# Attention steps of the next group spread over nine tenths of a group's MoE, with a larger planned sum of their matmuls

## The chip, the cores and the metric

The kernel runs on one core of one Trainium2 chip. The metric is the device time of one execution in microseconds, the median over several. A core has a matrix engine (TensorE, PE in the profile), a vector engine (VectorE, DVE), an activation engine (ScalarE, ACT), a general-purpose engine (GpSimd, POOL) and a queue engine (SyncE, SP). Each has its own instruction stream, and streams wait for one another through semaphores. Matmul results go to PSUM, from where ACT and DVE read them.

## The reference

Two stages: attention over 4 batches, 8 heads, 768 positions and head size 64, then a mixture of four experts (MoE) on its output.

```python
scores = scale * np.matmul(q, k.transpose(0, 1, 3, 2))
# retrieval heads 0, 2, 6: causal mask; the other five ("streaming" heads):
# causal and (key among the first 4, or within the last 64 positions)
a = softmax(where(mask, scores, -1e9))
attn = np.matmul(a, v)                      # x = attn as (3072, 512)

p = domain_probs / (domain_probs.sum(-1, keepdims=True) + 1e-09)
for e in range(4):
    h = np.maximum(x @ w1[e], 0.0)          # 512 -> 1024
    out += p[:, e:e + 1] * (h @ w2[e])      # 1024 -> 512
```

## The kernel before

The 3072 rows are cut into eight **groups** of 384 rows: group g is half c = g mod 2 of batch b = g div 2. Matrix operands are fp16. After the attention of group 0, the loop over g (line 783) runs the MoE of group g, and weaves the attention of group g + 1 into it.

**The MoE of a group** is the generator `moe_group` (line 716). For each of four experts it makes eight layer-1 tiles, each of four matmuls of 384 columns (line 728) into a PSUM buffer `pA`, which ACT empties with a Relu into `hs` (line 741). Then come three layer-2 tiles, each of eight matmuls of 512 columns (line 749) into a PSUM buffer `pO`, which DVE multiplies by the expert's weight and adds to `acc` (lines 761 and 765). The generator yields after every layer-1 tile and in the middle and at the end of every layer-2 tile. These places are called here A0 to A7 and B0a, B0b, B1a, B1b, B2a, B2b, with the expert ahead of them: e2A7 is the place after the last layer-1 tile of expert 2. The place at the end of a layer-2 tile comes after that tile's `acc` instruction has been issued, the one in its middle comes before.

**The attention of a group** is the generator `attention` (line 500), which yields in steps:

- S h.i, a score tile of head h: matmuls of q and k into a `pA` buffer (line 561), an Exp on ACT to `es` (line 579), a mask multiplication on DVE (line 583) where there is one. Then `run_late()` issues the DVE multiplications (line 633, "scale" below) that are still owed by heads finished earlier.
- V h.i, a part of the value product of head h into a `pV` buffer (line 609). After the last part of a head come a Ln (line 628) and an Exp (line 638) on ACT, which turn the row sums into reciprocals, and the head's scale, which writes the MoE's input `xT`, is put on the list `late`.
- T, only for group 1: a transposition of k or q by matmuls (line 457) into a `pA` buffer, with casts on DVE out of it. For later groups the SP queue does this by DMA transposes.

Heads alternate: the scores of head h are woven with the values of head h - 1. When the steps are used up, a last `run_late()` (line 690) issues the scales of heads 6 and 7. A retrieval head has 2 score tiles where c = 0 and 4 where c = 1; a streaming head has one (in groups 2 to 7).

**Buffers.** `pA` has four, shared in turn by layer-1 tiles, score tiles and transpositions; a tile that wants the buffer of four tiles earlier waits for the Relu, Exp or cast that reads it. `pO` and `pV` have two each.

**The pace** is set at lines 797 to 815. Each step and each MoE place has a planned matmul time, `mm_ns(cols)` = cols/2.4 + 2.5 ns per matmul; UNIT, an expert's, is 10,380 ns. After each MoE place, with `spent` MoE ns done, steps are taken

```python
            while done < (spent - begin) / (end - begin) * att_ns:
                step = next(att_steps, None)
```

so `end` is the point of the group's MoE at which `att_ns` of steps should be done. The steps' own planned sums are 9,037 ns for group 1 (`att_ns` is 6600 + 1100 + 1340 = 9040 there), 3,740 ns for groups 2, 4 and 6 (`att_ns` 3700), and 6,680 ns for groups 3, 5 and 7 (`att_ns` 6600).

**Queues.** POOL issues the loads of group g + 2 at the top of the loop (lines 788 to 795). SP gets the DMA transposes of group g + 2 when half of the MoE's planned time is spent (line 809), the copies of sink rows (`sink_rows`) when the first scores are made, and the output rows at the end of each group.

Of the kernel before, what the change touches and what calls it, by code (L numbers as in the profile page):

```python
# [17 lines left out]
def kernel(  # L18
# [32 lines left out]
    E, DM, F = moe_w1.shape  # L51
    CH = 3 * P
    NCH = S // CH
# [57 lines left out]
    def windows(x, c):  # L111

        return x[1 - c][:, 0 : WT * NSH * P].rearrange(
            "p (t s x) -> p t s x", t=WT, s=NSH
        )
# [67 lines left out]
    def load_q(b, c):  # L183
        q16[b, c] = att.tile([P, 3, H, D], FP16, name="q16", bufs=2)
        load_by_rows(q, q16[b, c], b, c)
# [10 lines left out]
    def load_k(b, c):  # L196

        for h in range(H):
            if RETR[h]:
                gp.dma_start(  # L200
                    out=kRr[:, RH.index(h), :, own(h)], in_=rows_of(k, b, h, c)
                )
            else:
                gp.dma_start(  # L204
                    out=kSr[:, :, SH.index(h), own(h)],
                    in_=windows_of(k, b, h, c),
                )
# [17 lines left out]
    def dma_transposes(b, c):  # L225
        i = b % 2
        put_sinks(kSr, k_sinks, c)
        alloc_qT(b, c)
        for j in range(3):
            nc.sync.dma_start(  # L230
                out=qTs[b, c][:, :, j * P : (j + 1) * P],
                in_=q16[b, c][:, j, :, :].rearrange("p h d -> p (h d)"),
                transpose=True,
            )
        for x, xr in ((kR[i][:, c, :, :, :], kRr), (windows(kSf, c), kSr)):
            nc.sync.dma_start(
                out=x.rearrange("p t s x -> p (t s) x"),
                in_=xr.rearrange("p t s x -> p (t s x)"),
                transpose=True,
            )  # L240

    def load_v(b, c, heads):
        for h in heads:
            t = v_tile(b, c, h)
            if RETR[h]:
                gp.dma_start(  # L246
                    out=t[:, 3 * c : 3 * c + 3, own(h)], in_=rows_of(v, b, h, c)
                )
            elif b:
                gp.dma_start(  # L250
                    out=t[:, :, own(h)], in_=windows_of(v, b, h, c)
                )
            else:
                gp.dma_start(
                    out=t[R0:P, TC * c : TC * (c + 1), own(h)],
                    in_=tiles_of(v, b, h, c),
                )
# [35 lines left out]
    def fill(eng, ap, value):  # L293
        ap = ap.bitcast(FP32)
        if eng is nc.scalar:
            src = ones[0 : ap.shape[0], :]
            if len(ap.shape) == 3:
                src = src.rearrange("p (a b) -> p a b", a=1)
            elif len(ap.shape) == 4:
                src = src.rearrange("p (a b c) -> p a b c", a=1, b=1)  # L300
            eng.copy(out=ap, in_=src.to_broadcast(list(ap.shape)))
        else:
            eng.memset(ap, value)
# [4 lines left out]
    def one_values_r(eng, i, c):  # L308
        t = slice(3 * c, 3 * c + 3)
        fill(eng, vR[i][:, t, :, D:P], ONES)  # L310
# [128 lines left out]
    def mm_ns(cols):  # L439
        return cols / 2.4 + 2.5  # L440
# [341 lines left out]
    UNIT = FTP * DMP * mm_ns(CH) + 3 * FTP * mm_ns(DM)  # L782
    for g in range(G):
        nxt = g + 1
        att_steps = iter(())
        if nxt < G:
            att_steps = attention(nxt // NCH, nxt % NCH)
        if g + 2 < G:
            b2, c2 = divmod(g + 2, NCH)
            load_k(b2, c2)  # L790
            load_q(b2, c2)
            if b2 == 1:
                one_values_r(gp, b2, c2)
                fill(gp, windows(vSf, c2).rearrange("p t s x -> p (t s x)"), ONES)
            load_v(b2, c2, range(H))

        begin = {0: 0.2, 1: 1.0}.get(g, 0.0) * UNIT
        end = {0: 2.2}.get(g, 0.93 * E) * UNIT

        att_ns = 3700.0 if nxt % NCH == 0 else 6600.0  # L800
        if nxt < NCH:
            att_ns += 1100.0 + 8 * 3 * mm_ns(P)
        spent = 0.0
        done = 0.0
        to_transpose = g + 2 < G
        for ns in moe_group(g):
            spent += ns
            if to_transpose and spent > 0.5 * E * UNIT:
                dma_transposes(*divmod(g + 2, NCH))
                to_transpose = False  # L810
            while done < (spent - begin) / (end - begin) * att_ns:
                step = next(att_steps, None)
                if step is None:
                    break
                done += step
        for _ in att_steps:
            pass
# [35 lines left out]
```

The softmax here doesn't subtract the row's maximum and nothing guards it: scores larger than these inputs give would overflow.

## Time and profile before

| | us |
|---|---|
| median of 6 executions | 414.83 (413.12, 413.12, 414.81, 414.84, 414.85, 414.86) |
| the profiled execution, its own time | 414.81 |
| its span, first to last instruction | 413.1 |
| PE busy in the span | 398.1 (96%) |
| ACT busy | 241.0 (58%) |
| DVE busy | 155.5 (38%) |
| mean granted TensorE clock | 0.995 |

The six times stand on two levels 1.7 us apart; the profiled execution is on the upper one. In the profile a matmul row's length is longer than the distance between the starts of two matmuls, because matmuls are pipelined; where PE stands is read from distances between starts. MoE groups begin at 24.29, 80.75, 126.52, 176.33, 221.99, 271.80, 317.46 and 367.27 us of the span (groups 0 to 7).

### The profile page before, as it was taken

What the parts mean: (1) busy time and instruction counts of PE and PEld (TensorE: products, weight loads), DVE (VectorE), ACT (ScalarE), POOL (GpSimd) and SP (SyncE); (2) the same over time, 40 slices, a digit from 0 to 9 for tenths busy, and PEclk for the clock granted to TensorE, in tenths of its full rate; (3) what the DMA queues carried; (4) which work ended last, traced back from release to release, by engine and by line L of the source; (5) the groups of instructions that cost most, each with busy time, mean ns of one, the idle gap of its engine ahead of it and who ended that gap; (6) DMA issues with size and microseconds to landing.
All of it is one profiled execution on the core that took longest, in us unless ns stands there. A gap on an engine that the chain in (4) does not pass through costs nothing.

```text
span 413.1 us, 6801 instructions
## 1 busy us (share of the span) xinstructions
PE 398.1 (96%) x2670; PEld 223.9 (54%) x2670; DVE 155.5 (38%) x302; ACT 241.0 (58%) x509; POOL 141.6 (34%) x176
## 2 busy tenths in 40 slices
PE   6899999999999999999999999999999999999995
PEld 3665555555555555555555555555555555555552
DVE  7875653223433325233333333233343222432222
ACT  2776874336876547656665448566565477653331
POOL 8938618459359168002930085000000000000000
PEclk9899999999999999999999999999999999999999
DMA  9999999999979999058984999259002000020002
GB/s 173 147 192 203 210 207 131 130 218 105 166 89 188 174 102 113 27 107 147 113 51 96 183 71 77 17 108 166 2 2 76 5 2 0 2 76 2 1 2 76
DMA packets 159988, 40.83 MB, mean 99 GB/s; under 512 B 150364, under 2 KB 154836, under 8 KB 159956
## 3 DMA queue, kind: packets, MB, share of 16 engines
q0 software_dynamic: 102592, 20.98, 62.9%
q1 hardware_dynamic: 54164, 18.62, 22.0%
q10 hardware_dynamic: 3200, 0.79, 0.9%
q8 instruction: 21, 0.34, 0.3%
q14 instruction: 11, 0.09, 0.1%
HBM read 43.57 MB, written 6.29 MB: 121 GB/s over the span
## 4 chain that ended last, share of the span: by engine, by line
PE 87%; ACT 7%; DVE 3%; issue 1%; DMA 1%; ACTq 0%; DVEq 0%
PE pO L749 40%; PE pA L728 36%; PE pV L609 5%; PE pA L561 5%; ACT hs L741 2%; ACT rc L628 2%; ACT rc L638 1%; ACT es L579 1%; DMA q<-in_q_dram 1%; DVE kS L490 1%; DVE vS L261 1%; DVE kR L474 1%; ACTq L328 0%; PE pA L454 0%; PE pO L355 0%
## 5 line engine op out<-in xcount | busy, mean ns | idle before, releaser
L728 PE MATMUL pA<-xT,w1sb 128*128 128x384 f16 x1024 | 187.4, 326 | 3.9 <-ACT hs L741 2.5
L749 PE MATMUL pO<-w2sb,hs 128*128 128x512 f16 x768 | 180.8, 379 | 0.0
L741 ACT ACTIVATE hs<-pA 128x384 f16<-128x384 f32 x256 | 122.1, 494 | 95.9 <-PE pA L728 89.0
L728 PEld LDWEIGHTS <-w1sb 128*128 128x128 f16 x1024 | 96.8, 98 | 65.5 <-issue 5.5
L749 PEld LDWEIGHTS <-hs 128*128 128x128 f16 x768 | 72.7, 98 | 74.2 <-ACT hs L741 0.6
L765 DVE SCALAR_TENSOR_TENSOR acc<-pO,p_sb,acc 128x512 f32<-128x512 f32 x72 | 53.9, 749 | 99.5 <-PE pO L749 98.8
L579 ACT ACTIVATE es<-pA 128x512 f16<-128x512 f32 (+3 forms) x122 | 61.1, 511 | 24.0 <-PE pA L561 20.9
L628 ACT ACTIVATE rc<-pV,eps 64x384 f32<-64x384 f32 x60 | 34.5, 575 | 33.0 <-PE pV L609 32.0
L250 POOL DMA_DIRECT2D vS<-in_v_dram x30 | 30.4, 1025 | 33.1 <-PE pV L609 32.7
L204 POOL DMA_DIRECT2D kSr<-in_k_dram x30 | 30.1, 1005 | 31.8 <-DMA kS<-kSr 12.1
L633 DVE TENSOR_TENSOR xT<-pV,rc 64x384 f16<-64x384 f32 x60 | 33.1, 552 | 4.2 <-PE pA L728 1.7
L583 DVE TENSOR_TENSOR es<-es,mW 128x384 f16<-128x384 f16 x30 | 10.8, 360 | 57.2 <-ACT es L579 57.2
L200 POOL DMA_DIRECT2D kRr<-in_k_dram x18 | 14.1, 783 | 53.1 <-DMA kR<-kRr 49.1
L638 ACT ACTIVATE rc<-rc 64x384 f32<-64x384 f32 x58 | 30.2, 521 | 1.8
L761 DVE TENSOR_SCALAR acc<-pO,p_sb 128x512 f32<-128x512 f32 x24 | 18.0, 749 | 34.3 <-PE pO L749 34.3
L583 DVE TENSOR_TENSOR es<-es,mC 128x256 f16<-128x256 f16 (+1 forms) x42 | 11.3, 268 | 45.4 <-ACT es L579 45.0
L561 PE MATMUL pA<-qT,kR 128*128 128x384 f16 (+2 forms) x120 | 25.2, 280 | 0.4
L609 PE MATMUL pV<-es,vR 128*128 128x384 f16 (+2 forms) x120 | 21.8, 280 | 0.0
L246 POOL DMA_DIRECT2D vR<-in_v_dram x24 | 19.2, 802 | 4.4 <-DMA w2sb<-in_moe_w_dram 4.3
L561 PEld LDWEIGHTS <-kS 128*128 128x128 f16 x255 | 14.0, 98 | 9.9 <-issue 3.2
L561 PE MATMUL pA<-qT,kS 128*128 128x55 f16 (+4 forms) x255 | 16.9, 196 | 2.4 <-ACT es L579 1.7
L609 PEld LDWEIGHTS <-vS 128*128 128x128 f16 x255 | 13.3, 98 | 7.5 <-DVE vS L261 1.4
(77 smaller groups left out, 162.7 us busy)
## 6 DMA issues: line engine op xcount, KB each, us to landing
out_dram<-acc SPq DMA_DIRECT2D x24, 256.0 KB
w1sb<-in_moe_w_dram POOLq DMA_DIRECT2D x4, 1024.0 KB, 14.9
w2sb<-in_moe_w_dram POOLq DMA_DIRECT2D x4, 1024.0 KB, 17.8
kSr<-in_k_dram POOLq DMA_DIRECT2D x30, 112.0 KB, 3.7
vS<-in_v_dram POOLq DMA_DIRECT2D x30, 112.0 KB, 4.0
q<-in_q_dram POOLq DMA_DIRECT2D x18, 128.0 KB, 4.2
vR<-in_v_dram POOLq DMA_DIRECT2D x24, 48.0 KB, 4.4
kRr<-in_k_dram POOLq DMA_DIRECT2D x18, 48.0 KB, 3.8
```

The source lines that it names most:

```text
L204: gp.dma_start(out=kSr[:, :, SH.index(h), own(h)], in_=windows_of(k, b, h, c),)
L250: gp.dma_start(out=t[:, :, own(h)], in_=windows_of(v, b, h, c))
L561: nc.tensor.matmul(out=ps[:, o : o + nq], lhsT=key_tile(b, c, h, t), rhs=qTs[b, c][:, hp, q0 : q0 + nq], start=(n == 0 or not first), stop ...
L579: nc.scalar.activation(out=es[:, 0:cols], in_=ps[:, 0:cols], func=AF.Exp, scale=SC)
L609: nc.tensor.matmul(out=ps[:, q0 : q0 + nq], lhsT=v_tile(b, c, h)[:, t, :], rhs=es[:, o : o + nq], start=(n == 0), stop=(n == len(work) - 1 ...
L628: nc.scalar.activation(out=rc[r, :], in_=ps[o, 0:CH], func=AF.Ln, bias=eps[o, :])
L633: nc.vector.tensor_tensor(out=xT[g][r, hp, :], in0=ps[r, 0:CH], in1=rc[r, :], op=ALU.mult)
L638: nc.scalar.activation(out=rc[r, :], in_=rc[r, :], func=AF.Exp, scale=-1.0)
L728: nc.tensor.matmul(out=pss[ft][:, 0:CH], lhsT=w1sb[:, e * DMP + ct, ft * P : (ft + 1) * P], rhs=xT[g][:, ct, :], start=(ct == 0), stop=(ct ...
L741: nc.scalar.activation(out=hs[:, ft, :], in_=ps[:, 0:CH], func=AF.Relu)
L749: nc.tensor.matmul(out=ps_o, lhsT=hs[:, ft, j * P : (j + 1) * P], rhs=w2sb[:, e * FTP + ft, :], start=(ft == 0), stop=(ft == FTP - 1),)
L765: nc.vector.scalar_tensor_tensor(out=acc[nt], in0=ps_o, scalar=p_ap, in1=acc[nt], op0=ALU.mult, op1=ALU.add,)
```

## The change

Two constants of the pace. The fraction of a group's MoE at which the steps should be done goes from 0.93 to 0.90 for every group but group 0, whose own `end` of 2.2 UNIT stays. The planned sum of the steps of groups 1, 3, 5 and 7 goes from 6600 to 6800 ns (for group 1, with the rest of its sum, from 9040 to 9240); the 3700 ns of groups 2, 4 and 6 stay.

```diff
         begin = {0: 0.2, 1: 1.0}.get(g, 0.0) * UNIT
-        end = {0: 2.2}.get(g, 0.93 * E) * UNIT
-
-        att_ns = 3700.0 if nxt % NCH == 0 else 6600.0
+        end = {0: 2.2}.get(g, 0.90 * E) * UNIT
+
+        att_ns = 3700.0 if nxt % NCH == 0 else 6800.0
         if nxt < NCH:
             att_ns += 1100.0 + 8 * 3 * mm_ns(P)
```

No instruction is added or removed. Worked out by the loop's own condition, steps come at another place; the table names those that the prediction speaks of, and others move by a place as well (an x marks the last part of a head, "end" the last `run_late()`):

| MoE of group | steps and their place before | place after |
|---|---|---|
| 0 | T3k and T3q (k and q of heads 6 and 7) e1A5, S4.0 e1A6, V6.2x e2A1, V7.0x e2A2 | T3k e1A4, T3q e1A5, S4.0 e1A6, V6.2x and V7.0x e2A1 |
| 1 | V5.0x e3A0, S6.1 e3A2, S7.0 e3A3, V6.0x e3A6, V7.0x e3B0b, end e3B1b | e2B2b, e3A1, e3A2, e3A4, e3B0a, end e3B0b |
| 2, 4, 6, expert 1 | V0.2x e0B2b, S2.0 A0, V1.0x A2, S2.1 A3, S2.2 A5, S2.3 A7, S3.0 B0a | V0.2x e0B2a, S2.0 e0B2b, V1.0x A1, S2.1 A2, S2.2 A4, S2.3 A6, S3.0 A7 |
| 2, 4, 6, expert 2 | V2.2x A1, S4.0 A2, V3.0x A3, S5.0 A5, V4.0x A7, S6.0 B0a, V5.0x B0b | V2.2x e1B2b, S4.0 A0, V3.0x A1, S5.0 A3, V4.0x A4, S6.0 A6, V5.0x B0a |
| 2, 4, 6, expert 3 | S6.3 A0, S7.0 A1, V6.0 A3, V6.1 A6, V6.2x and V7.0x B0b, end B1b | S6.3 and S7.0 in expert 2, V6.0 A0, V6.1 A2, V6.2x A6, V7.0x A7, end B0a |
| 3, 5 | V3.0x e2A0, S5.0 e2A3, V4.0x e2A6; V7.0x e3B0a, end e3B1b | V3.0x e1B2b, S5.0 e2A2, V4.0x e2A4; V7.0x e3A7, end e3B0b |

## Prediction

> **What bounds the kernel now.** I read the page first, then the PE's waits, then the MoE groups as windows, then the timeline where a group is longer than its work.
>
> ```profile
> PE 398.1 (96%) x2670; PEld 223.9 (54%) x2670; DVE 155.5 (38%) x302; ACT 241.0 (58%) x509; POOL 141.6 (34%) x176
> PE 87%; ACT 7%; DVE 3%; issue 1%; DMA 1%; ACTq 0%; DVEq 0%
> PE pA L728 <- ACT hs L741: 2.5, 4, 0.7
> ...
> 126.52:176.33 49.81, 48.84 (x337) 27.43 (x336) 16.16 (x31) 30.82 (x65) 26.00 (x29) 1.00 1.33 117
> 176.33:221.99 45.66, 45.66 (x314) 25.42 (x313) 16.17 (x32) 27.93 (x59) 17.27 (x19) 1.00 0.93 101
> 367.27:408.81 41.54, 41.54 (x225) 21.83 (x223) 9.30 (x13) 15.68 (x32) 0.00 (x0) 1.00 0.05 20
> ```
>
> PE bounds it, and the longest wait of PE in the woven part is for a Relu. The last group, which has nothing woven in, takes 41.54 us, so an expert costs 5.20 + 5.18. Group 2 (second column: its length) carries 6.68 of steps and 0.02 extra for each of 10 streaming products: 41.52 + 6.68 + 0.20 = 48.40, and 49.81 is 1.41 more. Only such excess can be won; the change moves steps, and their matmuls stay. Where it sits, group 2, expert 2, PE and ACT:
>
> ```profile
> 155.97 0.36 PE L561 MATMUL pA<-qT,kS 128*128 128x54 f16 x7
> 156.17 0.81 PE L728 MATMUL pA<-xT,w1sb 128*128 128x384 f16 x4
> 157.72 0.81 PE L728 MATMUL pA<-xT,w1sb 128*128 128x384 f16 x4 [0.73 <-ACT hs L741]
> ...
> 155.13 0.48 ACT L579 ACTIVATE es<-pA 128x384 f16<-128x384 f32 x1
> 155.50 0.50 ACT L741 ACTIVATE hs<-pA 128x384 f16<-128x384 f32 x1
> 156.03 0.57 ACT L628 ACTIVATE rc<-pV,eps 64x384 f32<-64x384 f32 x1
> 156.63 0.52 ACT L638 ACTIVATE rc<-rc 64x384 f32<-64x384 f32 x1
> 157.18 0.87 ACT L741 ACTIVATE hs<-pA 128x384 f16<-128x384 f32 x2
> ```
>
> Four matmuls need 0.65, so the start at 157.72 is 0.90 late: the Relu that frees the buffer ran only at 157.18, behind a Ln and an Exp. By the same reading the distances between starts are 0.28 and 0.27 too long at 141.96 and 143.54 (expert 1), and so in groups 4 and 6; in group 1, 0.15 and 0.18 at 117.03 and 117.84; in groups 3 and 5, 0.15 and 0.09. Group 0 loses 0.87 in all at 47.58 and 48.68, 1.03 at 51.34, 0.43 at 61.51.
>
> **How I cost a place.** ACT's spacing when it never rests, from this timeline: Relu 0.375 to the next start, Exp of 384 columns 0.375, of 512 columns 0.48, Relu to Ln 0.515 to 0.53, Ln to Exp 0.605, Exp to next 0.545. A Ln+Exp pair thus takes about 1.3. ACT starts 0.20 after the last matmul has been issued, PE 0.055 after the release (157.67 to 157.72). PE: a layer-1 tile 0.65, a streaming product 0.20, a layer-2 half 0.86. I walk PE and ACT forward in issue order, from an idle ACT, with four `pA` buffers in turn; times below run from the end of the MoE matmuls ahead of the stretch.
>
> **Groups 2, 4, 6, expert 1.** New order: S2.0, A0, A1, V1, A2, S2.1, A3, A4, S2.2, A5. ACT: Relu0 at 1.07, Relu1 1.72, Ln 2.24, Exp 2.84, Relu2 3.39 to 3.88, Exp of S2.1 to 4.36, Relu3 to 4.73. PE reaches S2.2 at 3.89 and waits for Relu2 until 3.94; A5 at 4.15 waits for S2.1's Exp until 4.41. Loss 0.04 + 0.26 = 0.30, against 0.55: gain 0.25 each.
>
> **Expert 2.** New order: V2.2x, A0, S4, A1, V3, A2, A3, S5, A4, V4, A5, A6, S6, A7. The first pair now begins at 0.31, beside layer 2, where ACT had been idle; the old order has all three pairs among the Relus. Relu0 1.46, Exp 1.84, Relu1 2.21, Ln 2.73, Exp 3.33, Relu2 3.88 to 4.37. A5, due at 4.16, waits until 4.42: 0.26. The third pair sits between Relu4 and Relu5, so Relu7 runs at 7.89 to 8.38, and the last matmul of layer 2's first tile, due at 8.30, waits to 8.44: 0.14. Loss 0.40 against 0.89: gain 0.49 each.
>
> **Expert 3.** Here the change adds a wait. V6.2x moves to A6, V7 to A7, and the last `run_late()` to B0a, so DVE gets the two scales ahead of the `acc` of the first layer-2 tile; before, they came after the second. From the end of A6's matmuls: Relu6 0.20, Ln 0.72, Exp 1.32, Relu7 1.87, Ln 2.38, Exp 2.99 to 3.51. Scale of head 7 at 3.56, `acc` at 4.12 to 4.87. The third layer-2 tile wants that `pO` buffer when PE has done V6 (0.11), A7 (0.65), V7 (0.20) and two tiles (3.45), at 4.41: it starts at 4.93, 0.52 late. Behind this `acc` waits only the next `acc`. That DVE keeps its issue order shows in group 0:
>
> ```profile
> 51.24 0.52 ACT L638 ACTIVATE rc<-rc 64x384 f32<-64x384 f32 x1
> ...
> 52.20 0.29 DVE L583 TENSOR_TENSOR es<-es,mS 128x256 f16<-128x256 f16 x1 [1.39 <-ACT es L579]
> 52.52 0.56 DVE L633 TENSOR_TENSOR xT<-pV,rc 64x384 f16<-64x384 f32 x1
> ```
>
> The scale's reciprocal was there at 51.76 and DVE idle, yet it ran after the mask issued ahead of it. Bounds of the new wait: 0, if the chain is 0.5 shorter than my walk, and 1.67, if it ends one pair (1.15 back to back) later. I take 0.52. The Trainium skill (PSUM — Partial Sum Buffer, Engine vs sequencer instructions) says that ScalarE and VectorE queues are strict first-in first-out; that speaks against this change, and without the rule the `acc` could pass the scales and the sum would be 411.7.
>
> Each such group: -0.25 - 0.49 + 0.52 = -0.22 (bounds -0.74 and +0.93); three: -0.66. My walk falls short of the old losses by 0.03 to 0.07 a group, so I take -0.60.
>
> **Group 1.** V5.0x's pair starts one layer-1 tile earlier, in layer 2: Relu0 1.55, Relu1 1.93 to 2.42, Exp of S6.1, Relu2. A3 waits 0.01; the 0.33 goes. -0.32 (bounds -0.33, 0).
>
> **Groups 3, 5.** V3.0x's pair also goes into layer 2, and the 0.09 goes; expert 1's 0.15 stays. The scales come after B0's `acc` (end at B0b), so no wait is added. -0.18 together (bounds -0.48, +0.2).
>
> **Group 0.** T3k comes 0.65 earlier than T3q, so its two casts of 0.80 hold a buffer that S4.0 and A7 wanted 0.65 earlier; of 0.87 some 0.55 goes. V6.2x and V7.0x now queue their pairs behind the same tile: up to 0.15 more than 0.43. -0.40 (bounds -0.87, and +0.6 if a tile waits for half a pair).
>
> **Other queues, at nothing.** The only DMA a step issues is the sink copy ahead of S0.0, whose place stays, so SP's order does too. POOL's load of vS at 173.35 waits for V7 (its idle 9.82 before it) and starts up to 1.7 earlier, then stops for the transposes until 188.16 as now. The waits of PE name no DMA after the first microseconds; were that cover gone, a load of about 4 us would show. `xT`, now complete at 176.61, 0.2 before the fourth matmul of group 3 wants it (176.34 + 0.49), will be so some 2.5 before the next group.
>
> **The sum.** -0.60 - 0.32 - 0.18 - 0.40 = -1.5. The profiled execution took 414.81 (span 413.1 and 1.7 around it), 0.02 under the median, so 413.3. The 0.375 between Relus is the trace's (0.87 for two from 157.18, the next start at 157.93). The Trainium skill (ScalarE: Activation LUTs, What ACT_TABLE_LOAD costs) gives an ACTIVATE with immediate operands 186 ns + 0.833 per element and lets neighbours overlap by 93, an estimate of 413 for 384 columns. By it six spacings put Relu7 of expert 2 back by 0.23, the 0.14 there would be 0.37 in three groups, the sum -0.8 and the time 414.0.
>
> **The rivals.**
>
> 1. No block at the end of the group (chance 0.15). For it: 0.52 rests on a chain of eight ACT spacings. Against it: six of them are seen above. Then 3 x 0.52 more is won: 411.7.
> 2. The collisions only move (0.11): new stalls of 0.1 to 0.3 in the dozens of moved steps, which a walk from an idle ACT understates, eat what is won. For it: groups 3 and 5 keep 0.15 whatever comes. Against: the losses found are all Ln+Exp pairs among Relus. 414.8.
> 3. Slower, by the `acc` behind the scales (0.18). Should head 7's reciprocal end one more pair later, each block is 1.67 and the sum -1.5 + 3 x 1.15 = +1.95: 416.8. It turns to slower by more than 0.3% from a block of 1.43. For it: DVE keeps its order, and only two `pO` exist. Against: ACT has only the Relus beside it in expert 3.
>
> **How the numbers follow.** The forecast has 0.56 and its own range is 412.4 to 414.2; 0.43 of it is faster by over 0.3% (1.24 us, about what a measurement of this kernel can tell from no change), 0.13 within. Rival 1 is faster, rival 2 within, rival 3 slower: 0.58, 0.24, 0.18. The range leaves out rival 3 and reaches from rival 1, less 0.4 because a median may fall on the lower of the two levels, to rival 2 plus 0.8: 411.3 to 415.6.
>
> **What would show it.** Right: groups 2, 4 and 6 last 49.6 instead of 49.81, with no 0.7 wait of PE for a Relu, and three waits of PE at line 749 for `acc` of about 0.5 some 2 us before a group ends; group 1 45.45, groups 3 and 5 45.57; group 1 begins at 80.35. Wrong: waits for `acc` over 1 us, or none, or a wait of PE for a DMA. The step I trust least is the 0.52.

## The result and the profile after

The changed kernel takes 413.34 us (median of 24), the kernel before 414.84 (median of 50 beside it): a ratio of 0.9966, 95% interval 0.9954 to 0.9977. The predicted time was 413.3.

The executions of every kernel here stand on two levels some 1.7 us apart (before 413.12 and 414.85, after 411.62 and 413.35), which part ahead of and at the start of group 0's MoE (it begins at 24.30 us of the span or at 22.88) and are alike from the second half of group 0 on, so below, upper level is compared with upper level, and lengths of groups with lengths of groups. Both profiled executions above are on the upper level.

The page after (busy time and the chain of work that ended last, by engine), PE's waits, and the windows of groups 1, 2, 3 and 7 (start and end, length, busy time by engine):

```profile
PE 396.7 (96%) x2670; PEld 222.4 (54%) x2670; DVE 156.0 (38%) x302; ACT 240.9 (59%) x509; POOL 141.7 (34%) x176
PE 83%; ACT 8%; DVE 4%; issue 2%; DMA 2%; DVEq 0%; ACTq 0%
```

```profile
PE pO L749 <- DVE acc L765: 1.1, 3, 0.4
...
PE pA L728 <- ACT hs L741: 0.4, 1, 0.4
```

```profile
79.98:125.43 45.45, 45.45 (x313) 25.38 (x312) 16.35 (x31) 27.99 (x59) 27.57 (x31) 1.00 1.39 147
125.43:175.17 49.74, 49.08 (x338) 27.38 (x337) 16.48 (x31) 31.02 (x65) 26.27 (x29) 1.00 1.32 120
175.17:220.75 45.58, 45.58 (x313) 25.35 (x312) 16.31 (x31) 27.93 (x59) 17.26 (x19) 1.00 0.92 99
365.79:407.31 41.52, 41.52 (x225) 21.81 (x223) 9.01 (x12) 15.70 (x32) 0.00 (x0) 1.00 0.05 18
```

The listed waits for a Relu have shrunk from 2.5 in four to 0.4 in one, in group 0 (shorter ones are not listed), and three waits for an `acc` are new. The number of matmuls is the same. PE's share of the chain fell from 87% to 83% while the time fell too: the chain tells through which engine the last work went, not how much was won. By group, from first layer-1 matmul to first layer-1 matmul:

| group | before | after | difference | predicted |
|---|---|---|---|---|
| 0 | 56.46 | 55.69 | -0.77 | -0.40 |
| 1 | 45.77 | 45.45 | -0.32 | -0.32 |
| 2, 4, 6 (each) | 49.82 | 49.73 | -0.09 | -0.20 |
| 3, 5 (each) | 45.65 | 45.58 | -0.07 | -0.09 |
| sum | | | -1.50 | -1.50 |

The spans differ by 1.5 as well (413.1 and 411.6). So the whole is right and two terms are not; their errors cancel.

**Group 0, expert 1** (PE and ACT of the kernel before, then PE of the changed kernel):

```profile
47.58 0.82 PE L728 MATMUL pA<-xT,w1sb 128*128 128x384 f16 x4
48.68 0.26 PE L561 MATMUL pA<-qT,kS 128*128 128x64 f16 x2 [0.28 <-ACT hs L741]
49.19 0.24 PE L561 MATMUL pA<-qT,kS 128*128 128x160 f16 x1 [0.25 <-DVE kS L490]
...
47.59 0.52 ACT L638 ACTIVATE rc<-rc 64x384 f32<-64x384 f32 x1
48.14 0.49 ACT L741 ACTIVATE hs<-pA 128x384 f16<-128x384 f32 x1
```

```profile
46.48 0.82 PE L728 MATMUL pA<-xT,w1sb 128*128 128x384 f16 x4
47.24 0.36 PE L457 MATMUL pA<-ident,q 128*64 128x128 f16 x6
47.53 0.82 PE L728 MATMUL pA<-xT,w1sb 128*128 128x384 f16 x4
48.26 0.34 PE L561 MATMUL pA<-qT,kS 128*128 128x64 f16 x3
```

Before, S4.0 starts 0.45 late and is held up by 0.41 once more. In the changed kernel it is 0.08 late, and T3q, which now stands behind a layer-1 tile of its own, 0.11.

**Group 2, expert 1** (PE, the changed kernel):

```profile
140.22 1.46 PE L728 MATMUL pA<-xT,w1sb 128*128 128x384 f16 x8
141.57 0.38 PE L561 MATMUL pA<-qT,kR 128*128 128x128 f16 x2
142.06 1.46 PE L728 MATMUL pA<-xT,w1sb 128*128 128x384 f16 x8
```

The score tile at 141.57 is 0.04 late, and the layer-1 tile at 142.06 is 0.27 late, 0.31 in all.

**Group 2, expert 2** (PE and ACT, start and length of each merged row):

```profile
154.19 0.36 PE L609 MATMUL pV<-es,vS 128*128 128x54 f16 x7
154.69 1.46 PE L728 MATMUL pA<-xT,w1sb 128*128 128x384 f16 x8
...
157.91 1.24 PE L749 MATMUL pO<-w2sb,hs 128*128 128x512 f16 x4
158.99 0.38 PE L561 MATMUL pA<-qT,kR 128*128 128x256 f16 x2
```

```profile
153.00 0.57 ACT L628 ACTIVATE rc<-pV,eps 64x384 f32<-64x384 f32 x1
153.60 0.52 ACT L638 ACTIVATE rc<-rc 64x384 f32<-64x384 f32 x1
154.14 0.87 ACT L741 ACTIVATE hs<-pA 128x384 f16<-128x384 f32 x2
```

The streaming product at 154.19 needs 0.20 (0.18 and the 0.02 extra), so the layer-1 tile after it is 0.30 late (0.32 with the extra). It is the pattern of the kernel before, a Relu behind a Ln and an Exp, but with one pair ahead of the Relu that counts instead of two. In layer 2 the four matmuls from 157.91 need 0.86, so the score tile at 158.99 is 0.22 late.

**Group 2, expert 3** (PE, ACT, DVE):

```profile
169.45 3.62 PE L749 MATMUL pO<-w2sb,hs 128*128 128x512 f16 x16
173.44 1.89 PE L749 MATMUL pO<-w2sb,hs 128*128 128x512 f16 x8 [0.37 <-DVE acc L765]
```

```profile
169.21 0.58 ACT L628 ACTIVATE rc<-pV,eps 64x384 f32<-64x384 f32 x1
169.82 0.52 ACT L638 ACTIVATE rc<-rc 64x384 f32<-64x384 f32 x1
170.37 0.49 ACT L741 ACTIVATE hs<-pA 128x384 f16<-128x384 f32 x1
170.88 0.57 ACT L628 ACTIVATE rc<-pV,eps 64x384 f32<-64x384 f32 x1
171.49 0.52 ACT L638 ACTIVATE rc<-rc 64x384 f32<-64x384 f32 x1
```

```profile
170.38 0.55 DVE L633 TENSOR_TENSOR xT<-pV,rc 64x384 f16<-64x384 f32 x1 [6.18 <-ACT rc L638]
172.04 0.56 DVE L633 TENSOR_TENSOR xT<-pV,rc 64x384 f16<-64x384 f32 x1 [1.12 <-ACT rc L638]
172.64 1.41 DVE L765 SCALAR_TENSOR_TENSOR acc<-pO,p_sb,acc 128x512 f32<-128x512 f32 x2
```

Sixteen matmuls from 169.45 need 3.45, so the next start, 173.44, is 0.53 late. The last matmul of the first layer-2 tile had been issued by 169.45 + 1.73 = 171.18, and DVE stood idle for 1.12 until 172.04; yet the `acc` came at 172.64, after the scale that had been issued ahead of it and that waited for head 7's Exp.

### The profile page after: what moved, and what is told of

The parts are those of the page before. It is cut to its first block, busy times and chain, and to the rows that moved or that the text cites. A ratio compares the mean times of both kernels' runs of the same rounds, so it can differ in the third digit from the quotient of the medians.

```text
span 411.6 us, 6803 instructions
## 1 busy us (share of the span) xinstructions
PE 396.7 (96%) x2670; PEld 222.4 (54%) x2670; DVE 156.0 (38%) x302; ACT 240.9 (59%) x509; POOL 141.7 (34%) x176
## 4 chain that ended last, share of the span: by engine, by line
PE 83%; ACT 8%; DVE 4%; issue 2%; DMA 2%; DVEq 0%; ACTq 0%
PE pO L749 38%; PE pA L728 35%; PE pA L561 4%; PE pV L609 4%; ACT rc L628 3%; ACT hs L741 2%; ACT rc L638 2%; DMA q<-in_q_dram 2%; ACT es L579 1%; DVE vS L261 1%; DVE kS L490 1%; DVE acc L765 1%; DVE qT L465 0%; PE pO L355 0%; DVE xT L633 0%
## 5 line engine op out<-in xcount | busy, mean ns | idle before, releaser
L583 DVE TENSOR_TENSOR es<-es,mW 128x384 f16<-128x384 f16 x30 | 10.8, 359 | 44.6 <-ACT es L579 44.5
```

## The experiments

Two theories. A, that of the prediction: what counts is where the Ln and Exp pairs fall among the Relus on ACT, and what stands ahead of an `acc` on DVE. B, the rival: what counts is that the attention is done earlier in a group, which frees buffers for the loads and completes `xT` sooner. The upper-level times and lengths of the traced execution:

| kernel | time, upper level | group 0 | 1 | 2, 4, 6 | 3, 5 |
|---|---|---|---|---|---|
| before | 414.85 | 56.46 | 45.77 | 49.82 | 45.65 |
| changed | 413.35 | 55.69 | 45.45 | 49.73 | 45.58 |
| 0.90 alone | 413.83 | 56.48 | 45.45 | 49.63 | 45.58 |
| 6800 alone | 414.06 | 55.39 (lower level) | 45.76 | 49.82 | 45.66 |
| scales behind the `acc` | 411.75 | 55.70 | 45.45 | 49.20 | 45.59 |
| group 0 as before | 414.11 | 56.48 | 45.45 | 49.73 | 45.59 |
| the tail alone | 416.42 | 56.15 (lower) | 45.77 | 50.35 | 45.65 |
| changed, no second Exp | 408.05 | 54.20 (lower) | 45.43 | 48.37 | 45.44 |
| before, no second Exp | 408.60 | 55.38 | 45.43 | 48.37 | 45.44 |
| two paces | 410.40 | 55.70 | 45.45 | 48.75 | 45.58 |
| two paces, 0.97 | 414.91 | 55.41 (lower) | 45.45 | 48.69 | 47.15 |

A group 0 of the lower level is 0.29 to 0.31 shorter where its steps fall at the same places. The times of the two kernels without the second Exp come from two executions each.

### The fraction alone

```diff
-        end = {0: 2.2}.get(g, 0.93 * E) * UNIT
+        end = {0: 2.2}.get(g, 0.90 * E) * UNIT
```

> The fraction 0.90 alone, with the old 6600. Theory A (where the Ln and Exp pairs fall among the Relus on ACT, and whether the scales of heads 6 and 7 stand ahead of an acc on DVE): groups 1, 3 and 5 as in the changed kernel (45.45, 45.58, 45.58), group 0 about as before (56.46, its planned sum is the old one); groups 2, 4 and 6 about 49.63 by the same walk, with two waits behind Relus (0.53 in expert 1, 0.67 in expert 2) and no wait for an acc, since heads 6 and 7 come later than in the changed kernel. Together about -1.1 against the kernel before. Theory B (the rival: what counts is only that the attention is done earlier in a group, so that xT and the buffers of the loads are free sooner): most of the -1.5 comes from the fraction, in every group alike, about 0.2 each.

Ratio to the kernel before 0.998 (0.9961 to 0.9998); on the upper level -1.02. Groups 2, 4 and 6 last 49.63, as the walk had it, with losses of 0.55 in expert 1 and 0.70 in expert 2 and no wait for an `acc`. They win 0.19 each; group 1 wins 0.32, groups 3 and 5 0.07. By B the gain would be alike everywhere, and it is not.

### The planned sum alone

```diff
-        att_ns = 3700.0 if nxt % NCH == 0 else 6600.0
+        att_ns = 3700.0 if nxt % NCH == 0 else 6800.0
```

> The planned sum 6800 alone, with the old 0.93. Theory A: group 0 as in the changed kernel (55.69, -0.77, its pace depends on the sum alone), groups 1, 3 and 5 as before (45.77, 45.65, 45.65), groups 2, 4 and 6 about 49.78 (0.53 in expert 1, 0.67 and 0.14 in expert 2, no wait for an acc). Together about -0.9. Theory B: the attention ends only 3 per cent earlier, in four of the groups, so less than -0.5, spread over groups 2, 4 and 6.

Ratio 0.9987 (0.9969 to 1.0005), which doesn't tell it from no change; on the upper level -0.79. Nearly all of it is group 0. Groups 2, 4 and 6 are unchanged at 49.82, 0.04 above what was expected (their losses are 0.55, 0.70 and 0.19, walked as 0.53, 0.67 and 0.14).

The two halves don't add up: 1.02 and 0.79 make 1.81, and the change brings 1.50. Only both together move heads 6 and 7 to e3A6 and e3A7, ahead of the first `acc`.

### The scales behind the acc

```diff
             yield from values(H - 1)
+            yield 120.0
         run_late()
```

> The changed kernel with a last planned step of 120 ns that does nothing, so that the scales of heads 6 and 7 are issued at e3B0b, behind the first acc, instead of at e3B0a ahead of it. Theory A: the three waits of PE for an acc (0.53 each) go, groups 2, 4 and 6 last 49.20 instead of 49.73, the rest stays: -1.6 against the changed kernel, about -3.1 against the kernel before. Theory B: xT is complete a little later, so no gain, 0 to +0.3 against the changed kernel.

Ratio 0.9925 (0.99 to 0.995); 1.60 below the changed kernel on the upper level. Group 2's window:

```profile
125.46:174.67 49.21, 48.92 (x338) 27.37 (x337) 16.48 (x31) 31.03 (x65) 26.17 (x29) 1.00 1.32 120
```

49.20 was expected, and PE's waits name no `acc` any more. The same place in the order of DVE's instructions cost 0.53 a group and nothing else.

### Group 0 at its old pace

```diff
-        att_ns = 3700.0 if nxt % NCH == 0 else 6800.0
+        att_ns = 3700.0 if nxt % NCH == 0 else (6600.0 if g == 0 else 6800.0)
```

> The changed kernel with the old planned sum in group 0 alone. Theory A, with what the trace of the changed kernel shows: group 0 is 56.46 again, the others as in the changed kernel: +0.77 against it, -0.73 against the kernel before. With the prediction's term for group 0 it would be +0.40. Theory B: group 0 should count like the others, about +0.2.

Ratio 0.9982 (0.9964 to 1.0); 0.76 above the changed kernel on the upper level, with group 0 at 56.48. So half of what the change brings is won in group 0, by the larger planned sum, and the prediction's 0.40 is too small.

### The new wait by itself

The kernel before, with this in its loop:

```diff
         for ns in moe_group(g):
             spent += ns
+            if g in (2, 4, 6) and spent > 3.3 * UNIT:
+                end, att_ns = 0.90 * E * UNIT, 6800.0
```

> The kernel before, with the changed pace only in the last part (from 3.3 UNIT on) of groups 2, 4 and 6: V6.1 comes at e3A4, V6.2x at e3A6, V7.0x at e3A7 and the last scales at e3B0a; all else is the kernel before. Theory A: the wait for an acc arises by itself, 0.53 in each of the three groups, which last 50.35 instead of 49.83: +1.6 against the kernel before, slower although the attention is done earlier. Theory B: earlier is better, 0 to -0.3.

Ratio 1.0035 (1.0016 to 1.0054), slower, by 1.57 on the upper level. A wait of PE and the window of group 2:

```profile
PE pO L749 <- DVE acc L765: 1.1, 3, 0.4
```

```profile
124.80:175.15 50.35, 49.01 (x337) 27.38 (x336) 16.44 (x31) 30.82 (x65) 27.29 (x31) 1.00 1.32 121
```

The attention is done earlier than in the kernel before and the kernel is slower: B falls.

### Both kernels without the second Exp

This leaves out the reciprocal of the row sums in groups 1 to 7: the heads are multiplied with the Ln.

```diff
-                nc.scalar.activation(out=rc[r, :], in_=rc[r, :], func=AF.Exp, scale=-1.0)
+                if first:
+                    nc.scalar.activation(
+                        out=rc[r, :], in_=rc[r, :], func=AF.Exp, scale=-1.0
+                    )
                 late.append(scale)
```

> The changed kernel without the second activation of a pair (the Exp that turns the Ln of the row sum into a reciprocal) in the attention of groups 1 to 7; the heads are multiplied with the Ln instead, so the reciprocal is left out. Theory A: a pair costs ACT about 0.6 instead of 1.15, and the losses of groups 1 to 6 go but for some 0.1: groups 1, 3, 5 about 45.47, groups 2, 4, 6 about 48.41, -4.0 against the changed kernel in these groups, with no wait for an acc. Theory B: as ACT is idle for more than a third of the time, little changes, -0.5 or less.

> The kernel before without the same Exp of groups 1 to 7 (the reciprocal is left out). Theory A: with the pairs halved it makes no difference to groups 1 to 6 where the steps fall, so these groups are as long as in the changed kernel without the Exp (45.47 and 48.41, within 0.1), and the two kernels differ in group 0 alone. Theory B: the changed kernel keeps its lead of about 0.1 to 0.3 in each of these groups.

Windows of groups 1 and 2, first of the changed kernel without the Exp, then of the kernel before without it:

```profile
77.07:122.50 45.43, 45.43 (x313) 25.34 (x312) 16.35 (x31) 24.86 (x51) 23.52 (x26) 1.00 1.45 145
122.50:170.87 48.37, 48.37 (x337) 27.45 (x336) 16.61 (x31) 27.08 (x57) 30.29 (x34) 1.00 1.45 131
```

```profile
79.67:125.10 45.43, 45.43 (x313) 25.34 (x312) 16.22 (x31) 24.68 (x51) 29.90 (x33) 1.00 1.36 149
125.10:173.47 48.37, 48.37 (x337) 27.45 (x336) 16.15 (x31) 26.87 (x57) 23.93 (x27) 1.00 1.27 118
```

The lengths agree to 0.01 although the steps fall at different places, and 48.37 is the bare work (41.52 + 6.68 + 0.20 = 48.40). Less than 4 us of ACT work in a group of nearly 50, taken off an engine that is busy for 31 of them, removes 1.4 of PE's time: ACT is short only in the stretches where a pair meets the Relus. With that gone the two kernels differ in group 0 alone. There 55.38 less the level's 0.31 is 55.07 against 54.20, a difference of 0.87; the two executions on the lower level, 406.88 and 405.99, differ by 0.89. (The one of 408.05 lies 2.06 above its kernel's other, more than the levels are apart, so the 0.55 between the table's two times is too small.)

### Two paces

```diff
-        end = {0: 2.2}.get(g, 0.90 * E) * UNIT
+        end = {0: 2.2}.get(g, (0.90 if g % 2 else 0.95) * E) * UNIT
-        att_ns = 3700.0 if nxt % NCH == 0 else 6800.0
+        att_ns = 3700.0 if nxt % NCH == 0 else (6800.0 if g == 0 else 6600.0)
```

> The changed kernel with a pace of its own for groups 2, 4 and 6: 0.95 and 6600, so their attention ends later than in both kernels; group 0 keeps 6800, groups 1, 3 and 5 keep 0.90 and 3700. Theory A: by the walk of PE and ACT groups 2, 4 and 6 lose 0.25 in expert 1 and nearly nothing else, 48.75 instead of 49.73, and no wait for an acc: -2.9 against the changed kernel, -4.4 against the kernel before, about 410.4. Theory B: a later end costs, slower than the changed kernel and than the kernel before in these groups.

Ratio to the kernel before 0.9892 (0.9864 to 0.992); 4.45 below it and 2.95 below the changed kernel on the upper level. It is the fastest of the kernels that leave nothing out. Windows of groups 2 and 3:

```profile
125.45:174.20 48.75, 48.63 (x337) 27.36 (x336) 16.11 (x31) 30.93 (x65) 27.38 (x31) 1.00 1.38 123
174.20:219.79 45.59, 45.59 (x314) 25.36 (x313) 16.60 (x32) 27.95 (x59) 17.27 (x19) 1.00 0.96 103
```

The attention of groups 3, 5 and 7 now ends later than in either kernel, and 48.75 leaves 0.35 above the bare work.

### A little later still

Against the kernel with two paces:

```diff
-        end = {0: 2.2}.get(g, (0.90 if g % 2 else 0.95) * E) * UNIT
+        end = {0: 2.2}.get(g, (0.90 if g % 2 else 0.97) * E) * UNIT
```

> The kernel with two paces, with 0.97 instead of 0.95 for groups 2, 4 and 6. Heads 6 and 7 end at e3B1b instead of e3B1a, and the last scales come at e3B2b, behind the last acc of the group. Theory A: groups 2, 4 and 6 themselves stay at 48.7 to 48.8, but the group after each starts with a wait of about 1.56 of its first layer-1 tile for xT (groups 3 and 5 last 47.2 instead of 45.58, group 7 1.56 longer): +4.7 against 0.95, about level with the kernel before (414.8 where that is 414.8). A further theory C (now that the two paces won: the later the attention ends, the better, because ACT has more time): 0 to -1 against 0.95.

Ratio 0.9993 (0.9971 to 1.0015): the 4.5 are lost again. Groups 2, 4 and 6 even last 0.06 less than with 0.95, but the groups after them begin with a wait (group 3, PE and DVE):

```profile
172.44 0.65 PE L728 MATMUL pA<-xT,w1sb 128*128 128x384 f16 x3
...
172.64 0.75 DVE L765 SCALAR_TENSOR_TENSOR acc<-pO,p_sb,acc 128x512 f32<-128x512 f32 x1 [1.28 <-PE pO L749]
173.31 1.13 DVE L633 TENSOR_TENSOR xT<-pV,rc 64x384 f16<-64x384 f32 x2
...
174.49 0.32 PE L728 MATMUL pA<-xT,w1sb 128*128 128x384 f16 x1 [1.40 <-DVE xT L633]
```

Three matmuls from 172.44 need 0.49, so the fourth, which reads the last quarter of `xT`, is 1.56 late, as expected. Theory C falls.

## Why the prediction was right, point by point

**The sum and the time** (413.3, measured 413.34) are right, and so is the mechanism. The walk gave 48.75 for two paces and 1.56 for the wait for `xT` before those kernels had run, and they came out at that; the 0.53 of the wait for an `acc`, taken off one kernel and added to another, gave the 49.20 and 50.35 that were then measured. That the sum agrees to 0.05 is luck: groups 2, 4 and 6 won 0.33 less than their term, and group 0 won 0.37 more.

**Groups 1, 3 and 5** came as predicted (-0.32; -0.07 each for -0.09). The waits at e3A3 of group 1 and in expert 2 of groups 3 and 5 are gone, and the 0.15 in expert 1 of groups 3 and 5 stayed, as said.

**Groups 2, 4 and 6** are a mis-sized term: -0.20 each was taken, -0.09 measured. By its parts: expert 1 lost 0.56 before and loses 0.04 + 0.27 = 0.31 (gain 0.25, as said); expert 2 lost 0.90 and loses 0.30 + 0.22 = 0.52 (gain 0.38, said 0.49); expert 3 loses 0.53 (said 0.52). These losses make 1.36, which is what the group's 49.73 has above the 48.37 that it takes without the second Exp. It is expert 2 that was too good: its two waits were sized 0.04 and 0.08 too short. I took ACT's spacings at their shortest; in the changed kernel several are 0.01 to 0.03 longer (Relu to Ln 0.53 at 152.47, 0.54 at 155.27, for 0.515), and the last Relu ran 0.06 later than in the walk. The allowance from -0.66 to -0.60 for the three groups was meant for this and was too small. That the scales behind one another add the wait in expert 3 was right to 0.01, and it was the term I trusted least.

**Group 0** is the other mis-sized term: -0.40 was taken, -0.77 measured, and its own run gave 0.76. Its two items came out as sized. The 0.87 at T3 and S4.0 became 0.19, and T3k and T3q apart take 0.12 more than together, which makes a gain of 0.56 where I had 0.55; the extra wait in expert 2 is 0.14 (0.57 for 0.43), as bounded. What was left out is the rest: 0.29 in the first tiles of expert 1 (0.23 ahead of 42.63 and 0.06 ahead of 43.50), which went altogether, and 0.07 of the 1.03 at V4.0. My reason for the 0.87 was only half right, too. I had put it all to the casts, but the first 0.45 ended with a Relu, which ran at 48.14 behind a Ln and an Exp; only the 0.41 at 49.19 ended with a cast.

**Other queues at nothing** was right: no wait of PE names a DMA beyond the opening, and the POOL load that follows V7 moved without effect, by 2.3 (from 46.8 after the start of its group to 44.5) where I had said up to 1.7.

**The rivals.** No block at the group's end would have given 411.7, and the kernel without the block does take 411.75; the block was there. That the collisions only move is false, since no stalls came in groups 1 to 6 beyond those walked, and without the second Exp all the losses of groups 1 to 6 go. The slower rival needed 1.43 a group; the wait is 0.53.

**The two rules of the Trainium skill.** PSUM — Partial Sum Buffer, Engine vs sequencer instructions, says that VectorE's queue is first-in first-out; the trace agrees, with 1.12 of idle DVE ahead of a scale that stood before an `acc` whose last matmul had been issued by 171.18. ScalarE: Activation LUTs, What ACT_TABLE_LOAD costs, would space two ACTIVATEs of 384 columns by an estimate of 413 ns; here it is 0.375 to 0.38 (154.14 to 154.90 for two), and its 414.0 was further off than 413.3. Of the wait in layer 2 of expert 2, 0.22, the trace's spacing gave 0.14 and the page's 0.37.

## What to carry to other kernels

When the bounding engine runs in issue order at full rate, write down its loss against bare work by stage, and look for the few places where another engine, idle on the whole, is short for a microsecond: here a Ln and Exp pair of 1.3 among Relus of 0.375. Such losses can be walked through by hand from a handful of spacings, and the walk finds better places for the work as well as it explains the old ones. A multiplication that waits for a slow chain must not be issued ahead of one that frees a buffer, and finishing early is worth nothing by itself: 0.95 with a later end beat 0.90 by 2.95 us, and 0.97 gave it all back.

## What the runs showed of the hardware that was not expected

The two levels of the times. They are decided in the attention of group 0. In the executions of the upper level, here the changed kernel, DVE's copy of sink rows at line 261 (4 partitions by 256) shows

```profile
12.89 1.57 DVE L261 COPY vS<-vS 4x256 f16<-4x256 f16 x1
15.73 2.72 DVE L261 COPY vS<-vS 4x256 f16<-4x256 f16 x1
19.66 0.35 DVE L261 COPY vS<-vS 4x256 f16<-4x256 f16 x2
```

and in those of the lower level, here the tail alone,

```profile
12.21 0.71 DVE L261 COPY vS<-vS 4x256 f16<-4x256 f16 x1
14.19 0.27 DVE L261 COPY vS<-vS 4x256 f16<-4x256 f16 x1
15.77 2.75 DVE L261 COPY vS<-vS 4x256 f16<-4x256 f16 x2
```

In both, a copy that takes 0.21 undisturbed begins near 15.75 and lasts until about 18.5; meanwhile POOL runs its memsets, from 15.24 to 19.1 in the kernel before. What differs is how many of the copies had been done by then. The long copies end at fixed times, whenever they began: from 15.73 in the changed kernel and from 16.24 in the kernel before without the Exp to 18.45, and from 12.89 and 13.99 to 14.46. Each of these ends follows the end of a POOL instruction by less than 0.1: a memset from 17.14 to 18.37, and the issue of a load,

```profile
13.51 0.90 POOL L189 DMA_DIRECT2D q<-in_q_dram  x1
```

So it looks as if POOL's instructions hold the copies. No run moved either, so the cause stays open; by estimate, moving that work is worth up to the 1.7 us between the levels, more than the change studied here.
